# Linear attention and a GELU feed-forward layer: 192 bytes more ahead of one moving operand

## The chip, the cores and the metric

The kernel runs on 1 core of one Trainium2 chip, in one launch. The metric is device time in microseconds of that core, the median of the runs of a kernel.

## The reference

```
kv  = einsum('bhsd,bhse->bhde', k, v)          # 8 batches, 8 heads, seq 576, head_dim 64
out = einsum('bhsd,bhde->bhse', q, kv)
x   = out / sqrt(mean(out*out, -1) + 1e-6) * g_norm      # then heads side by side: (4608, 512)
h   = x @ w_in                                  # (512, 2048)
y   = gelu(h) @ w_out                           # (2048, 512); result (4608, 512)
```

All data are float32. The kernel splits each operand of the feed-forward layers into a high and a low part (hi and lo), and a product is hi·hi + lo·hi + hi·lo, three matmuls.

## The kernel before, in words

The 4608 tokens are cut into nine chunks of 512 (c = 0 to 8). The first two (PLAIN = 2) use the plain first layer, `layer1`. From c = 2 on the first layer uses Strassen's scheme with seven products per pair of feed-forward blocks: `layer1_pair` computes two of the 16 blocks of 128 features at once. One call of it is a *pair slot*; there are 7 chunks x 8 pairs = 56 of them. In a slot, `product(k, ...)` is called for k = 0 to 6, and each product issues 6 matmuls of 256 columns: two halves kb of the contraction, and for each the three terms (w hi, x hi), (w lo, x hi), (w hi, x lo). So a slot has 42 matmuls, all on line 444, and 56 slots have 2352. After a slot come the matmuls of the second layer (line 563, 512 columns), with the projections of the next chunk (line 218) between them in some slots. The order of the work is written out by hand (`manual_schedule`); the tile framework adds the waits.

A matmul has a *stationary* operand (weights, loaded into the array by an LDWEIGHTS of 128 columns, on the trace PEld) and a *moving* operand (streamed through, on the trace PE). While one matmul streams, the weights of the next are loaded. In `product` the weights come from a ring of four tiles w_in0 to w_in3, which the DMA queue of SyncE fills from DRAM (`load_products`), and the moving operand is `at.x[k]`, made by `high_block` (ScalarE cast, hi) and `low_block` (lo). For product 0 it lies in tile x2 (even c) or x0 (odd c); for product 1 in x3 or x1; for the others in tiles of the w_in family (`piece_tile`).

Where the operands lie is part of the program. The ring tiles have 64 elements (256 bytes) of room, and their contents start 48 elements (192 bytes) into the tile:

```
AWAY, ROOM = 48, 64
ring[t] = kept[t % RING][:, AWAY:AWAY + 2 * DM]
```

All other tiles start their contents at their first byte. As the program is built, the tiles named here begin, in each partition, at a byte address that leaves 192 when divided by 256 (x0 157888, x2 166080, w_in0 58560, w_in1 62912, w_in2 71360, w_in3 92096; the w_out, gh, gl and q tiles too). Pieces inside them begin at multiples of 512 bytes. In this text the *distance* of two operands is the start of the weights minus the start of the moving operand, taken modulo 256 bytes. It is 192 in all 42 matmuls of a slot, for a matmul's own weights and for the next ones alike; it is 0 in the second layer.

On the way to the prediction's steps: line 748 multiplies by an identity matrix (tile `ident`) at the start of the program; line 481 (`load_w`) issues the loads of the weights, w_in10 as the twentieth; lines 563 and 584 are the second layer and its very last part (`finish`), where the last row block is done in two halves of 256 columns.

Of the kernel before, what the change touches and what calls it, by code (L numbers as in the profile page):

```python
# [8 lines left out]
F32 = mybir.dt.float32  # L9
F32R = mybir.dt.float32r  # L10
# [6 lines left out]
P = 128  # L17
EPS = 1e-6
CH = 512
# [3 lines left out]
HALF = CH // 2  # L23
# [12 lines left out]
def linear_attn_rms_gelu_ffn(  # L36
# [16 lines left out]
    nc = tc.nc  # L53
    ctx.enter_context(tc.manual_schedule())
    NT, DM = out.shape
    B, NP = kv_main.shape[:2]
# [4 lines left out]
    NF = w_in.shape[0]  # L61
# [4 lines left out]
    const = ctx.enter_context(tc.tile_pool(name="const", bufs=1))  # L66
# [6 lines left out]
    HI, LO = slice(0, DM), slice(DM, 2 * DM)  # L73
    kv_h = [const.tile([P, NP, P], F32R, name=f"kv_h{s}") for s in range(2)]
    kv_l = [const.tile([P, NP, P], F32R, name=f"kv_l{s}") for s in range(2)]
    ident = const.tile([P, P], F32, name="ident")
    fold = const.tile([P, P], F32, name="fold")
    half_g = const.tile([P, 1], F32, name="half_g")
    heads = const.tile([P, 2], F32, name="heads")

    AWAY, ROOM = 48, 64

    def block_tile(name, dtype):
        ring = name in [f"w_in{i}" for i in range(RING)]
        return const.tile([P, 2 * DM + (ROOM if ring else 0)], dtype, name=name)


    kv_in, late = {}, {}  # L90

    def late_tile(name):

        if name not in late:
            late[name] = const.tile([P, 2 * DM], I32, name=name).bitcast(F32)
        return late[name]
# [77 lines left out]
    class Attn:  # L174
# [122 lines left out]
            self.low_x(p, eng)  # L297

        def high_x(self, p):
            x = const.tile([P, 2, CH], F32R, name=f"x{(NP * self.c + p) % 6}")  # L300
            nc.scalar.copy(out=x[:, 0], in_=self.o[p])
            self.x[p] = x

# [29 lines left out]
        def high_block(self, n):  # L333

            x = piece_tile(self.c, n)
            nc.scalar.copy(out=x[:, 0], in_=self.block(OPERANDS[n]))  # L336
            self.x[n] = x

        def low_block(self, n, eng=nc.gpsimd):
            x = self.x[n]  # L340
            eng.tensor_tensor(  # L341
                out=x[:, 1], in0=self.block(OPERANDS[n]), in1=x[:, 0].bitcast(F32),
                op=ALU.subtract,
            )

# [2 lines left out]
    OPERANDS = ((0, 0), "T1", "T2", "T4", (1, 0), (1, 1), "T3")  # L348
# [4 lines left out]
    def reused(i, dtype=F32):  # L353

        if i not in kept:
            kept[i] = block_tile(f"w_in{i}", dtype)
        return kept[i][:, :2 * DM]

    def piece_tile(c, n):
        k = (["x2", "x3"] + [f"w_in{i}" for i in range(5, 10)],  # L360
             ["x0", "x1", "x4", "x5"] + [f"w_in{i}" for i in range(10, 13)])[c % 2][n]
        return const.tile([P, 2, 2, HALF], F32R, name=k)

    products = [dram.tile([P, 2 * DM], F32, name=f"products{t}") for t in range(NT2)]

# [35 lines left out]
    def high_sums():  # L401

        for (j, second), s in stage.items():
            if j % 2:
                t = reused(second, F32R).rearrange("p (k a n) -> p k a n", k=2, a=2)
            else:
                t = const.tile([P, 2, 2, HALF], F32R, name=f"x{2 + second}")
            nc.scalar.copy(out=t[:, :, 0], in_=s)
            halved[j, second] = s, t
        stage.clear()  # L410
# [12 lines left out]
    def load_products(t):  # L423
        if t < (NCH - PLAIN) * NT2:
            reused(t % RING, F32R)
            ring[t] = kept[t % RING][:, AWAY:AWAY + 2 * DM]
            nc.sync.dma_start(out=ring[t].bitcast(F32), in_=products[t % NT2])

    def layer1_pair(at, j, between):


        a, b = (ps_h.tile([P, CH], F32, name="ps_h") for _ in range(2))
        left, right = slice(0, HALF), slice(HALF, CH)
        u = reused(15).rearrange("p (a n) -> p a n", n=HALF)
        p1, u2, v, u3 = (u[:, i] for i in range(4))
        add = lambda out, x, y: nc.vector.tensor_tensor(out=out, in0=x, in1=y, op=ALU.add)  # L436

        def product(k, out, first=False):
            n = ((at.c - PLAIN) * NF // 2 + j) * NPR + k
            w, x = ring[n // 2][:, n % 2 * DM:(n % 2 + 1) * DM], at.x[k]  # L440
            for kb in range(2):
                hi, lo = (w[:, m * HALF + kb * P:m * HALF + (kb + 1) * P] for m in range(2))
                for i, (y, z) in enumerate(((hi, 0), (lo, 0), (hi, 1))):
                    nc.tensor.matmul(  # L444
                        out=out, lhsT=y, rhs=x[:, z, kb], start=first and kb + i == 0,
                        stop=kb == 1 and i == 2, skip_group_check=True,
                    )
            if n % 2:
                load_products(n // 2 + RING)

        between[0]()
        product(0, a[:, left], True)
        product(1, a[:, right])
        nc.vector.tensor_copy(out=p1, in_=a[:, left])  # L454
        add(v, a[:, right], p1)
        product(2, b[:, right], True)
        product(3, b[:, left])
        add(u2, b[:, right], p1)
        between[1]()
        product(4, a[:, left])  # L460
        product(5, a[:, right])
        add(a[:, right], a[:, right], u2)
        product(6, b[:, right])
        add(u3, b[:, right], p1)
        add(b[:, left], b[:, left], u3)
        add(b[:, right], b[:, right], v)
        return a, b
# [9 lines left out]
    def load_w(n):  # L477
        kind, i = weights[n]
        src = w_in[i] if kind == "in" else w_out[i * P:(i + 1) * P, :]
        raw[n] = block_tile(f"w_{kind}{i}", I32)[:, :2 * DM]  # L480
        nc.sync.dma_start(out=raw[n], in_=src.bitcast(I32))
# [30 lines left out]
    def high_w(n):  # L512
        kind, i = weights[n]
        t = block_tile(f"w_{kind}{i}", F32R)[:, :2 * DM]
        parts[kind, i] = t
        nc.scalar.copy(out=t[:, HI], in_=ws[n].bitcast(F32))
# [90 lines left out]

    attn = [Attn(c) for c in range(NCH)]
    first, second = attn[:2]
    warm = late_tile(f"w_in{NF - 6}")[:, DM + P:DM + 2 * P]  # L610
    nc.vector.memset(warm, 0.0)
    nc.scalar.activation(out=heads, in_=warm[:, :2], func=AF.Gelu)
# [45 lines left out]
    for d in range(0, 2 * D, BLK):  # L658
        h = d // D * D
        nc.gpsimd.tensor_tensor(  # L660
            out=fold[:, d:d + BLK], in0=ident[:, h:h + BLK], in1=ident[:, h + BLK:h + 2 * BLK],
# [25 lines left out]
    n = 2 * NB  # L687


    def sum_squares(p):  # L690
# [10 lines left out]
        out=sums[:, :n + 4 * NG], lhsT=ones, rhs=eps[:, :n + 4 * NG], start=True, stop=False,  # L701
# [6 lines left out]
        out=half_g, in0=ps[:, :1], scalar1=0.5, scalar2=None, op0=ALU.mult  # L708
# [3 lines left out]
        out=root_g, in0=half_g, scalar1=D ** 0.5, scalar2=None, op0=ALU.mult  # L712
# [8 lines left out]
    for p in (2, 3):  # L721
# [5 lines left out]
        out=sums[:, :n].rearrange("p (g b) -> p g b", g=2), lhsT=fold, rhs=first.part[:, :2, :],  # L727
        start=False, stop=True, skip_group_check=True,
    )
    sum_squares(3)  # L730
    for p in (2, 3):
        nc.scalar.activation(
            out=first.o_tile(p), in_=first.ps.pop(p), func=AF.Copy, scale=root_g
# [9 lines left out]
    for p in (2, 3):  # L743
        bcs[p] = ps_acc.tile([P, DM], F32, name=f"acc{p}")
        for t in range(NG):
            for h, r in enumerate((slice(0, D), slice(D, 2 * D))):
                k = n + 2 * ((p - 2) * NG + t) + h
                nc.tensor.matmul(  # L748
                    out=bcs[p][r, t * P:(t + 1) * P],
                    lhsT=first.inv[:, k:k + 1].broadcast_to((P, D)), rhs=ident,  # L750
                    start=True, stop=True,
                )
    for p in range(2):
# [3 lines left out]
            out=first.o_tile(p), in0=first.ps.pop(p), scalar=root_g, in1=bc, op0=ALU.mult,  # L757
# [72 lines left out]
    def sum_weights(i, n, gelu_rest):  # L830

        high_sums()
        for k in range(n):
            if k:
                high_sums()
            combine(*halves.pop(0))
            if not k:
                gelu_rest()
            low_sums()
        if not n:  # L840
            gelu_rest()
            low_sums()
# [53 lines left out]
    for s in range(PLAIN * NF):  # L896
        c, i = divmod(s, NF)
# [35 lines left out]
        else:  # L933
# [3 lines left out]
            n = 0 if not 1 <= i <= 11 else 2 if i in (1, 3, 5, 7, 11) else 1  # L937
# [114 lines left out]
```

## Time and profile before

| | |
|---|---|
| median of 3 runs | 831.37 us (830.35 to 833.76) |
| the profiled execution, its own time | 831.25 us |
| its span, first to last instruction | 829.5 us |
| TensorE matmuls busy | 824.6 us (99% of the span) |
| weight loads busy (beside the matmuls) | 731.4 us (88%) |
| VectorE, ScalarE, GpSimd busy | 496.3, 314.0, 65.7 us |

The span is what the trace covers; 1.75 us of the execution's own time lie around it. A matmul's duration in the trace is longer than its pace, since matmuls are pipelined: what counts is the time from one start to the next.

### The profile page before, as it was taken

The numbers are of one execution on the slowest core, as the hardware profiler recorded it, in microseconds if no ns is written. First come the engines' busy times: TensorE is split into PE (matmuls) and PEld (weight loads), VectorE is DVE, ScalarE is ACT, GpSimd is POOL, SyncE is SP. The second block draws the span as 40 slices with busy tenths as digits, with TensorE's granted clock in tenths as the row PEclk, the third lists the DMA queues.
The fourth block names the chain that finished last, engine by engine and source line by source line (L and its number), as shares of the span: only waits on it lengthen the run. The fifth ranks groups of instructions, "written<-read, shape, count | busy, mean of one in ns | idle before, by whom it ended". The sixth has DMA issues, their size and how long they took to land.

```text
span 829.5 us, 13801 instructions
## 1 busy us (share of the span) xinstructions
PE 824.6 (99%) x5386; PEld 731.4 (88%) x5386; DVE 496.3 (60%) x980; ACT 314.0 (38%) x578; POOL 65.7 (8%) x69
## 2 busy tenths in 40 slices
PE   9999999999999999999999999999999999999998
PEld 7788888888999999999999999999999989999997
DVE  3899848677546744675457544673467456744443
ACT  3788544344431333233423253233423332322221
POOL 1000021002010100010100100010101000100000
PEclk9999999999999999999999999999999999999999
DMA  9981337777584578555845678456455655556551
GB/s 352 406 332 51 115 95 262 252 261 260 211 305 149 179 236 317 179 178 203 312 171 179 203 266 289 143 172 231 172 177 178 225 205 178 178 178 228 178 178 51
DMA packets 61605, 174.97 MB, mean 211 GB/s; under 512 B 6500, under 2 KB 15460, under 8 KB 61540
## 3 DMA queue, kind: packets, MB, share of 16 engines
q1 hardware_dynamic: 61536, 174.09, 60.4%
q8 instruction: 43, 0.70, 0.3%
q14 instruction: 22, 0.18, 0.1%
q10 hardware_dynamic: 4, 0.00, 0.0%
HBM read 149.95 MB, written 24.12 MB: 210 GB/s over the span
## 4 chain that ended last, share of the span: by engine, by line
PE 99%; DVE 0%; issue 0%; ACT 0%; DVEq 0%
PE acc L563 47%; PE ps_h L444 33%; PE ps_h L537 10%; PE ps_a L218 3%; PE ps_a L158 3%; PE ps_h L529 1%; PE ps_h L647 1%; PE acc L681 1%; PE acc L748 0%; PE ps_h L692 0%; PE ps_a L248 0%; DVE w L602 0%; DVE w_in L673 0%; PE ps_h L700 0%; DVE sq L591 0%
## 5 line engine op out<-in xcount | busy, mean ns | idle before, releaser
L563 PE MATMUL acc<-w_out,gh 128*128 128x512 f32 x700 | 216.7, 391 | 0.0
L444 PE MATMUL ps_h<-w_in,w_in 128*128 128x256 f32 x1392 | 173.0, 279 | 0.0
L444 PEld LDWEIGHTS ps_h<-w_in,w_in 128*128 128x128 f32 x1392 | 167.8, 188 | 0.0
L563 PE MATMUL acc<-w_out,w_in 128*128 128x512 f32 x672 | 159.3, 391 | 0.0
L563 PEld LDWEIGHTS acc<-w_out,gh 128*128 128x128 f32 x700 | 129.2, 188 | 25.3
L563 PEld LDWEIGHTS acc<-w_out,w_in 128*128 128x128 f32 x672 | 123.9, 188 | 24.6
L563 PE MATMUL acc<-w_out,gl 128*128 128x512 f32 x350 | 136.3, 389 | 0.0
L549 ACT ACTIVATE gh<-ps_h 128x512 fp32r<-128x512 f32 x88 | 52.7, 599 | 209.6 <-DVE ps_h L436 151.9
L444 PEld LDWEIGHTS ps_h<-x,w_in 128*128 128x128 f32 x960 | 120.9, 188 | 4.3
L444 PE MATMUL ps_h<-x,w_in 128*128 128x256 f32 x960 | 122.2, 279 | 0.0
L454 DVE COPY w_in<-ps_h 128x256 f32<-128x256 f32 x56 | 23.8, 425 | 131.6 <-PE ps_h L444 131.6
L549 ACT ACTIVATE w_in<-ps_h 128x512 fp32r<-128x512 f32 x56 | 33.6, 600 | 182.0 <-DVE ps_h L436 182.0
L436 DVE TENSOR_TENSOR ps_h<-ps_h,w_in 128x256 f32<-128x256 f32 x168 | 72.7, 433 | 46.1 <-PE ps_h L444 42.3
L436 DVE TENSOR_TENSOR w_in<-ps_h,w_in 128x256 f32<-128x256 f32 x168 | 71.4, 425 | 46.8 <-PE ps_h L444 44.9
L537 PE MATMUL ps_h<-x,w_in 128*128 128x512 f32 x360 | 86.8, 390 | 0.0
L555 DVE TENSOR_TENSOR gl<-ps_h,gh 128x512 fp32r<-128x512 f32 x88 | 60.4, 687 | 43.0 <-ACT ps_h L550 38.7
L550 ACT ACTIVATE ps_h<-ps_h 128x512 f32<-128x512 f32 x144 | 85.5, 594 | 0.0
L537 PEld LDWEIGHTS ps_h<-x,w_in 128*128 128x128 f32 x360 | 67.4, 188 | 13.9 <-POOL x L306 0.2
L563 PEld LDWEIGHTS acc<-w_out,gl 128*128 128x128 f32 x350 | 65.7, 188 | 13.9
L555 DVE TENSOR_TENSOR w_in<-ps_h,w_in 128x512 fp32r<-128x512 f32 x56 | 38.4, 686 | 17.1 <-ACT ps_h L550 17.1
L206 POOL TENSOR_TENSOR ql<-q,qh 128x512 fp32r<-128x512 f32 x16 | 21.3, 1331 | 210.6 <-ACT qh L205 152.9
L341 POOL TENSOR_TENSOR w_in<-o,w_in 128x512 fp32r<-128x512 f32 x13 | 17.0, 1325 | 208.1 <-ACT w_in L336 208.1
(153 smaller groups left out, 644.1 us busy)
## 6 DMA issues: line engine op xcount, KB each, us to landing
w_in<-products SPq DMA_DIRECT2D x196, 512.0 KB, 4.6
products<-w_in SPq DMA_DIRECT2D x40, 256.0 KB, 3.2
w_in<-w_in SPq DMA_DIRECT2D x16, 512.0 KB, 10.2
kv_main<-kv_main SPq DMA_DIRECT2D x16, 512.0 KB, 7.1
w_out<-w_out SPq DMA_DIRECT2D x16, 512.0 KB, 10.2
q<-qT SPq DMA_DIRECT2D x15, 512.0 KB, 6.0
out<-w SPq DMA_DIRECT2D x18, 256.0 KB, 2.1
out<-z SPq DMA_DIRECT2D x17, 256.0 KB, 2.3
```

What stands on the lines that cost most here:

```text
L158: nc.tensor.matmul(out=ps[r, n * D:(n + 1) * D], lhsT=k[:, r], rhs=v[:, r], start=(j == 0), stop=(j == NJ),)
L206: eng.tensor_tensor(out=ql, in0=q, in1=qh.bitcast(F32), op=ALU.subtract)
L218: nc.tensor.matmul(out=ps[:, a:e], lhsT=w, rhs=x[:, a:e], start=(m == 0), stop=(m == 2))
L341: eng.tensor_tensor(out=x[:, 1], in0=self.block(OPERANDS[n]), in1=x[:, 0].bitcast(F32), op=ALU.subtract,)
L436: add = lambda out, x, y: nc.vector.tensor_tensor(out=out, in0=x, in1=y, op=ALU.add)
L444: nc.tensor.matmul(out=out, lhsT=y, rhs=x[:, z, kb], start=first and kb + i == 0, stop=kb == 1 and i == 2, skip_group_check=True,)
L454: nc.vector.tensor_copy(out=p1, in_=a[:, left])
L537: nc.tensor.matmul(out=h, lhsT=parts["in", i][:, w][:, p * P:(p + 1) * P], rhs=at.x[p][:, x], start=(m + p == 0), stop=(m == 2 and p == NP ...
L549: nc.scalar.activation(out=gh, in_=h, func=AF.Gelu)
L550: nc.scalar.activation(out=h, in_=h, func=AF.Gelu)
L555: nc.vector.tensor_tensor(out=gl, in0=h, in1=gh.bitcast(F32), op=ALU.subtract)
L563: nc.tensor.matmul(out=ps, lhsT=x[:, ts], rhs=parts["out", i][:, w], start=(i == 0 and m == 0), stop=(m == 2 and (i == NF - 1 or (i, t) == ...
```

## The change

The tiles x0 and x2 get 64 more elements (256 bytes). When a tile holds the first product's operand (`n == 0` in `piece_tile`), its hi part starts 48 elements into the tile, with a gap of 16 elements between its two halves kb, and its lo part starts at element 576. So hi kb = 0 begins at byte 192, hi kb = 1 at byte 1280, lo at bytes 2304 and 3328: only the first of these four quarters leaves another remainder modulo 256. The operand becomes a pair of slices (`x[0]`, `x[1]`) in place of one tile with an axis for hi and lo. The 512 bytes that the two tiles take come from `ident`, which has no tile of its own any more: it lies in a part of w_in10 that is unused until that tile's weights are loaded.

```diff
-    ident = const.tile([P, P], F32, name="ident")
...
+    def x_tile(i):
+        return const.tile([P, 2 * DM + (ROOM if i in (0, 2) else 0)], F32R, name=f"x{i}")
...
         def high_x(self, p):
-            x = const.tile([P, 2, CH], F32R, name=f"x{(NP * self.c + p) % 6}")
+            x = x_tile((NP * self.c + p) % 6)[:, :2 * CH].rearrange("p (a n) -> p a n", a=2)
...
         def high_block(self, n):
             x = piece_tile(self.c, n)
-            nc.scalar.copy(out=x[:, 0], in_=self.block(OPERANDS[n]))
+            nc.scalar.copy(out=x[0], in_=self.block(OPERANDS[n]))
...
     def piece_tile(c, n):
         k = (["x2", "x3"] + [f"w_in{i}" for i in range(5, 10)],
              ["x0", "x1", "x4", "x5"] + [f"w_in{i}" for i in range(10, 13)])[c % 2][n]
-        return const.tile([P, 2, 2, HALF], F32R, name=k)
+        t = const.tile([P, 2 * DM], F32R, name=k) if k[0] == "w" else x_tile(int(k[1]))
+        if n:
+            hi, lo = t[:, :DM], t[:, DM:2 * DM]
+        else:
+            hi, lo = t[:, AWAY:AWAY + DM + 2 * (ROOM - AWAY)], t[:, DM + ROOM:]
+        return tuple(a.rearrange("p (k n) -> p k n", k=2)[:, :, :HALF] for a in (hi, lo))
...
                     nc.tensor.matmul(
-                        out=out, lhsT=y, rhs=x[:, z, kb], start=first and kb + i == 0,
+                        out=out, lhsT=y, rhs=x[z][:, kb], start=first and kb + i == 0,
...
+    ident = late_tile(f"w_in{NF - 6}")[:, DM + 2 * P:DM + 3 * P]
```

No instruction is added, removed or moved on any engine. In the built program the x0 and x2 tiles, the w_in tiles and the w_out tiles lie 512 bytes (x1 and x2: 256 bytes) lower than before, so their remainders modulo 256 stay at 192. The distances of a slot's 42 matmuls after the change: 0 for the first two (w hi and w lo with x hi, kb = 0), 192 for the other 40. Two kinds of wait change: the load of w_in10 waits for the last matmul of line 748 instead of an earlier one, and for GpSimd's work on `fold` instead of its memsets before. In seven ScalarE casts (`high_block(0)`, once a chunk) the output is two pieces of 256 elements with a gap.

## Rows read from the trace of the kernel before

**Rows 1.** The page: busy time, granted clock by slices, the chain that ended last.
```profile
PE 824.6 (99%) x5386; PEld 731.4 (88%) x5386; DVE 496.3 (60%) x980; ACT 314.0 (38%) x578; POOL 65.7 (8%) x69
...
PEclk9999999999999999999999999999999999999999
...
PE 99%; DVE 0%; issue 0%; ACT 0%; DVEq 0%
PE acc L563 47%; PE ps_h L444 33%; PE ps_h L537 10%; PE ps_a L218 3%; PE ps_a L158 3%; PE ps_h L529 1%; PE ps_h L647 1%; PE acc L681 1%; PE acc L748 0%; PE ps_h L692 0%; PE ps_a L248 0%; DVE w L602 0%; DVE w_in L673 0%; PE ps_h L700 0%; DVE sq L591 0%
```
**Rows 2.** Timeline of PE, first pair slot: start us, us, engine, line, operation, count.
```profile
209.78 0.39 PE L563 MATMUL acc<-w_out,gl 128*128 128x512 f32 x1
210.01 1.57 PE L444 MATMUL ps_h<-x,w_in 128*128 128x256 f32 x12
211.42 3.70 PE L444 MATMUL ps_h<-w_in,w_in 128*128 128x256 f32 x30
214.95 0.25 PE L218 MATMUL ps_a<-qh,kv_h 128*128 128x192 f32 x1
```
**Rows 3.** Timeline of PE, a slot of the last chunk.
```profile
737.42 1.58 PE L444 MATMUL ps_h<-x,w_in 128*128 128x256 f32 x12
738.83 3.69 PE L444 MATMUL ps_h<-w_in,w_in 128*128 128x256 f32 x30
742.36 0.63 PE L563 MATMUL acc<-w_out,gh 128*128 128x512 f32 x2
```
**Rows 4.** Stretches of line 444: length, PE busy, PEld busy, granted clock, DMA share, GB/s.
```profile
209.90:214.80 4.90, 4.79 (x41) 4.86 (x42) 1.00 0.40 116
737.30:742.20 4.90, 4.78 (x41) 4.86 (x42) 1.00 0.45 118
```
**Rows 5.** Timeline of PE, the last matmuls of the program.
```profile
824.65 0.40 PE L584 MATMUL acc<-w_out,gh 128*128 128x256 f32 x2
824.88 0.28 PE L584 MATMUL acc<-w_out,gl 128*128 128x256 f32 x1
825.00 0.40 PE L584 MATMUL acc<-w_out,gh 128*128 128x256 f32 x2
825.24 0.28 PE L584 MATMUL acc<-w_out,gl 128*128 128x256 f32 x1
825.36 0.40 PE L584 MATMUL ps_h<-w_out,gh 128*128 128x256 f32 x2
...
825.96 0.28 PE L584 MATMUL ps_h<-w_out,gl 128*128 128x256 f32 x1
```
**Rows 6.** Timeline of PE, projections of 256 columns (first and last of six).
```profile
301.43 0.28 PE L218 MATMUL ps_a<-qh,kv_h 128*128 128x256 f32 x1
...
302.02 0.28 PE L218 MATMUL ps_a<-ql,kv_h 128*128 128x256 f32 x1
```
**Rows 7.** Timeline of PE, second layer right behind a projection.
```profile
215.72 0.62 PE L563 MATMUL acc<-w_out,gh 128*128 128x512 f32 x2
...
217.11 0.62 PE L563 MATMUL acc<-w_out,gh 128*128 128x512 f32 x2
...
217.79 0.62 PE L563 MATMUL acc<-w_out,gh 128*128 128x512 f32 x2
```
**Rows 8.** Timelines of PE (identity matmuls) and of the SyncE queue (load of w_in10).
```profile
19.74 2.15 PE L748 MATMUL acc<-ident,y 128*64 128x128 f32 x32
...
38.74 0.33 SPq L481 DMA_DIRECT2D w_in<-w_in  x1
```
**Rows 9.** ACT groups, shapes apart: busy us, mean ns, idle before and releaser.
```profile
L336 ACT CAST x<-o 128x512 fp32r<-128x512 f32 x14 | 8.7, 619 | 13.1 <-DVE o L289 12.6 <-ACT ps_h L550 0.5
...
L408 ACT CAST x<-w 128x512 fp32r<-128x512 f32 x8 | 4.8, 610 | 4.2 <-DVE w L398 4.2
```

More of the change, by code (lines that the diff above doesn't have):

```diff
@@ L341, in low_block @@
             eng.tensor_tensor(
-                out=x[:, 1], in0=self.block(OPERANDS[n]), in1=x[:, 0].bitcast(F32),
+                out=x[1], in0=self.block(OPERANDS[n]), in1=x[0].bitcast(F32),
                 op=ALU.subtract,
@@ L406, in high_sums @@
             else:
-                t = const.tile([P, 2, 2, HALF], F32R, name=f"x{2 + second}")
+                t = x_tile(2 + second)[:, :2 * DM]
+                t = t.rearrange("p (k a n) -> p k a n", k=2, a=2)
             nc.scalar.copy(out=t[:, :, 0], in_=s)
```

## The prediction

> **What bounds the kernel now.** I read the page first. TensorE's matmuls are busy for 824.6 of 829.5 us, and the chain that ended last is 99% TensorE, 33% of the span of it on line 444, the matmuls of the pair slots [rows 1]. The granted clock is at its upper level, 2.4 GHz, in every slice of the page, and 1.00 in the stretches of two slots [rows 1, 4]. So the time is the sum of the paces at which TensorE starts its matmuls. A change that moves no instruction can act in two ways: through that pace, or through a new wait on TensorE.
>
> The pace is read from starts in the timeline. In the first slot 12 matmuls on the x tiles (products 0 and 1) take from 210.01 to 211.42, 1.41 us or 117.5 ns each; the 30 of products 2 to 6 take from 211.42 to 214.95, 3.53 us or 117.7 ns each. The whole slot is 4.94 us, 117.6 ns a matmul [rows 2]. A slot of the last chunk gives the same: 1.41 us, then 3.53 us, 4.94 us in all [rows 3]. 56 slots of 4.94 us are 276.6 us, one third of the span, as the chain says. The reader is to see in this how even it is. The matmuls that the change touches stand in the first group of 12, and that group is no slower than the other 30: there is no stall at the head of a slot that a better address could take away. It shows a second thing: products 0 and 1 read their weights from the first ring tile and the others from three more, which lie at different multiples of 256 bytes, and the pace is the same. That is why I count addresses modulo 256.
>
> **What the distance is worth, from rows.** The change takes the distance from 192 to 0 for two of a slot's 42 matmuls, 2 x 56 = 112 in all. Do matmuls of 256 columns run at another pace at distance 0? The slots don't show it, but the very last part of the program does: on line 584 the weights gh, gl and the moving w_out both begin at remainder 192. Its first two intervals go from 824.65 to 824.88, 0.23 us or 115 ns each. From there nine intervals go to 825.96, 1.08 us or 120.0 ns each [rows 5]. So distance 0, coming out of a run of 512-column matmuls as a slot does, starts a little faster than a slot's 117.6 and settles a little slower. The counterpart at distance 192 is on line 218: the kv tiles begin at remainder 128, the q tiles at 192, so the distance is 192 too, and five intervals from 301.43 to 302.02 take 0.59 us, 118 ns each, as in a slot [rows 6].
>
> Line 584 has other tiles than a slot, so this is the nearest row and no direct proof. By it each distance has a pace that it settles to, 117.6 at 192 and 120.0 at 0, and the way there lasts a few matmuls.
>
> **The Trainium skill against this.** The page "TensorE: Matmul & The Clock Gate", section "Step-by-step: what each phase is for", says that TensorE has two independent read ports, one for the moving operand and one for the weights, and that loading the next weights takes no read bandwidth from the matmul that runs. By that rule no distance matters, the change is worth nothing, and the time stays at 831.4 us. The rows differ from it by 2.4 ns a matmul (120.0 against 117.6), a hint and no more; no run here has yet put one operand at two distances. I keep the rule as a rival.
>
> **The terms of the sum.**
> 1. The two matmuls at distance 0. The head of a slot takes 2 x 117.6 = 0.235 us now. Bounds: 0.23 us, if it goes as the head of line 584, or 0.240 us, at the settled 120.0 ns [rows 2, 5]. Over 56 slots that is -0.28 to +0.27 us. I take -0.3 us, because the situation (two matmuls right behind 512-column ones) is that of the head of line 584.
> 2. What the other 40 do after that. If the pace depends on distance and on what went before, the disturbance can go on for some matmuls. How long such a thing lasts is shown by the second layer: right behind a projection, six intervals of 512-column matmuls go from 215.72 to 217.11, 1.39 us, while the next three take 0.68 us, 226.7 ns each, so that six settled ones take 1.36 us [rows 7]. The disturbance costs 0.03 us and is gone after six matmuls. As much at every slot, with either sign, is 56 x 0.03 = 1.7 us. I take 0: line 218 comes out of another kind of neighbour and is at 118 ns at once [rows 6], and a slot is too. The 1.7 us stay in the range.
> 3. The load of w_in10 now waits for the identity matmuls. They end at 19.74 + 2.15 = 21.89 us; that load is issued at 38.74 us [rows 8], 16.9 us later, in a queue that is behind older loads. Cost 0. Were the cover gone, the load and those behind it in the queue would be late by the difference.
> 4. The identity matmuls get another address as well: 2.15 us for 32 [rows 8]. At 5 ns each way they give 0.16 us at most; I take 0.
> 5. Seven casts write two pieces. The cast takes 619 ns; one on line 408, which already writes two separated pieces, takes 610 [rows 9], and ScalarE is busy 38% of the span [rows 1]. Cost 0; 10 ns more would hide in the 13.1 us for which ScalarE waits ahead of such casts.
> 6. The other tiles move by 256 or 512 bytes, and no remainder changes. Cost 0, by the four ring tiles above.
>
> Sum: -0.3 us on the execution's own 831.25, that is 830.95. The median of the runs shown stands 0.12 above it, so the forecast is 831.1 us. The runs shown spread from 830.35 to 833.76; half a per cent, 4.2 us, is about what a measurement can tell from no change, and I use it as the bound of "same".
>
> **Rivals.**
> *The head of the slot sets the pace of the whole slot (faster).* If the two matmuls at distance 0 put the weight loads and the stream into another alignment, and distance 192 holds that alignment, the fast pace of the head of line 584 could last: 115 against 117.6 ns for 42 matmuls is 0.11 us a slot, 6.1 us, giving 825.1 us. For it speaks that one and the same distance does show two paces, 115 at first and 120 later, so there is a memory [rows 5, 7]. Against it: in every stretch I read, the memory fades within about six matmuls, and 56 slots and line 218 all stand at the same pace after different neighbours. It counts as faster from 4.2 us / 2352 matmuls = 1.8 ns each, a slot of 4.87 us or less.
>
> *The settled pace of distance 0 holds for the slot (slower).* The same mechanism with the other sign: the slot goes on at 120.0 ns, 42 x 2.4 ns = 0.10 us a slot, 5.6 us over 56, giving 837.0 us. For it: 120.0 is the pace at which nine intervals in a row stand [rows 5]. Against it: 40 of 42 matmuls keep distance 192, whose settled pace is 117.6, and two at distance 0 have not yet got to 120 on line 584. It decides from 119.4 ns a matmul, a slot of 5.02 us.
>
> *The distance does nothing (same).* Rows 2, 3 and 6 are then simply what matmuls of 256 columns take, and line 584 is slower for another reason; 831.4 us. By the page's rule above it would be this.
>
> **How the numbers follow.** The forecast, with terms 1 and 2, has 0.60; that distance does nothing has 0.14; both lie within 0.5% and make "same" 0.74. The fast slot has 0.18: that a fast alignment exists is seen, that it lasts is not. The slow slot has 0.08. The likeliest case's own range is 831.1 with 1.7 us of term 2 and the spread of medians, 829 to 833.6. To leave out no more than 2 in 10 the range must reach one of the other cases; the fast slot is the likelier, so it goes down to 825.0; the slow one is left out.
>
> **What would show it.** In the timeline of the changed kernel the first slot's 12 matmuls on x tiles should take 1.40 to 1.42 us and the next 30 3.53; the granted clock should stay 1.00 there, and no wait should stand ahead of line 444. Right about the head but wrong about the rest would be a group of 30 that takes 3.45 us (115 ns) or 3.60 us (120 ns). The prediction is wrong if the pace of all 42 changes by 1.8 ns or more, which the memory after a short disturbance would have to carry over 40 matmuls; or if the time moves in a place that these rows don't speak of.

## The result, and the profile after

The changed kernel is slower: 834.40 us (median of 8 runs, 832.82 to 836.51) against 831.25 us (8 runs), a ratio of 1.0038 with a 95% interval of 1.0021 to 1.0055. The forecast was 831.1 us, in a range of 825.0 to 833.6, with "same" (less than half a per cent) as the likeliest. By that bound the outcome is still "same", but it is slower clear of the noise, and the time lies outside the range. Measured again beside the experiments below, the same kernel gave 833.13 against 830.97 us, 1.0027 (1.0013 to 1.0042), which lies inside it.

The page of the changed kernel (rows that answer to [rows 1]):

```profile
span 833.7 us, 13801 instructions
...
PE 828.7 (99%) x5386; PEld 733.0 (88%) x5386; DVE 496.0 (59%) x980; ACT 314.1 (38%) x578; POOL 65.6 (8%) x69
...
PE 97%; DMA 2%; SPq 0%; DVE 0%; issue 0%; ACT 0%; DVEq 0%
```

The span is 4.2 us longer, and TensorE is still busy for 99% of it. The 2% of the chain on DMA come from the one wait of TensorE that is new, 0.22 us for a load of kv_main at the start of the program:

```profile
18.23 1.12 PE L161 MATMUL ps_a<-kv_main 112*64 112x64 f32 x16 [0.22 <-DMA kv_main<-kv_main]
```

From the first slot on TensorE waits for nothing, before and after. So the question is again at which pace TensorE starts its matmuls, and where it got slower. The timeline of PE answers, first at the first pair slot (as [rows 2]; line 444 is now 454, line 563 is 573):

```profile
212.05 0.39 PE L573 MATMUL acc<-w_out,gl 128*128 128x512 f32 x1
212.28 1.57 PE L454 MATMUL ps_h<-x,w_in 128*128 128x256 f32 x12
213.69 3.69 PE L454 MATMUL ps_h<-w_in,w_in 128*128 128x256 f32 x30
217.22 0.25 PE L221 MATMUL ps_a<-qh,kv_h 128*128 128x192 f32 x1
```

Two things stand there. The slot starts 2.27 us later than before (212.28 against 210.01): that much of the 4.2 us was lost before any slot had used an operand at a new distance. And the slot is as long as before: 1.41, then 3.53 us, 4.94 in all. The other 2 us must have been lost between slots.

They were lost right behind them. A slot of the last chunk that is followed by 13 matmuls of the second layer in one row shows it. The kernel before:

```profile
768.60 1.58 PE L444 MATMUL ps_h<-x,w_in 128*128 128x256 f32 x12
770.01 3.69 PE L444 MATMUL ps_h<-w_in,w_in 128*128 128x256 f32 x30
773.54 3.12 PE L563 MATMUL acc<-w_out,w_in 128*128 128x512 f32 x13
```

The changed one, same slot:

```profile
772.59 1.57 PE L454 MATMUL ps_h<-x,w_in 128*128 128x256 f32 x12
774.00 3.70 PE L454 MATMUL ps_h<-w_in,w_in 128*128 128x256 f32 x30
777.53 3.17 PE L573 MATMUL acc<-w_out,w_in 128*128 128x512 f32 x13
```

The slot takes 4.94 us in both, and the same 13 matmuls behind it, whose operands the change does not touch, take 3.17 us in place of 3.12. Resolved into single intervals, from one start to the next in the two traces, in ns (the head as a mean of the 56 slots; the slot's last interval and the second layer behind it for the slot shown):

```
                    head of a slot (mean of 56)         last  second layer behind it
before              117.4 118.3 117.5 117.5 118.3 ...   115   233 231 226 227 227 226 227 227 226 227 227
changed             115.8 118.4 117.5 117.5 117.5 ...   118   241 237 233 236 224 231 236 228 233 231 226
```

The first interval of a slot is 1.6 ns shorter; after it the slot keeps the old pace, 117.8 ns in the mean. But the second layer now needs ten intervals to settle at 226.7 ns, where it needed two. Summed over the trace by stretches, the 56 slots are 0.14 us shorter and the stretches behind them 2.12 us longer: 55 to 56 ns behind each of the 35 slots that are followed at once by the second layer or by projections of 256 columns, 49 ns behind 3 where these have 512 columns, and next to nothing (-11 to +10 ns) behind the 18 slots where other work follows. From the first slot's first matmul to the last matmul's start it is 617.94 us against 615.95, 1.99 us or 0.24%.

The other 2.3 us belong to the start, and to the executions that were profiled. The identity matmuls, in the changed kernel's two profiled executions (the first in the result, the second among the experiments):

```profile
20.22 3.68 PE L759 MATMUL acc<-w_in,y 128*64 128x128 f32 x32
```
```profile
18.23 1.97 PE L759 MATMUL acc<-w_in,y 128*64 128x128 f32 x32
```

and the windows around them, with the granted clock behind the count; the third is of the kernel before, whose identity matmuls took 2.15 us [rows 8]:

```profile
18.00:22.00 4.00, 3.78 (x42) 0.50 1.03 405
```
```profile
18.00:22.00 4.00, 3.96 (x38) 1.00 1.04 409
```
```profile
18.00:22.00 4.00, 4.00 (x57) 0.73 1.02 399
```

In the first, TensorE ran this stretch at the lower clock, 1.2 GHz (0.50); in the second at 2.4 GHz (1.00); the kernel before had both (0.73). The first two had short waits for data ahead of it: TensorE was busy for 3.87 and 3.90 of the 4.00 us from 10 to 14 us. The same program shows both starts, so the lower clock does not come with the program. It makes the spreads wide: the five runs of the first measurement at a mean clock of 1.00 lie at 832.8 to 833.3 us but for one at 836.5, the three at 0.996 at 835.5 to 836.4. Whether the change makes such a start more frequent is open: the mean granted clock was 0.998 or less in 8 of 20 executions of the changed kernel, and in 13 of the 58 of the kernel before beside the experiments.

### The profile page after: what moved, and what is told of

Its sections match the earlier page's. It is cut to its first block, busy times and chain, and to the rows that moved or that the text cites. A ratio compares the mean times of both kernels' runs of the same rounds, so it can differ in the third digit from the quotient of the medians.

```text
span 833.7 us, 13801 instructions
## 1 busy us (share of the span) xinstructions
PE 828.7 (99%) x5386; PEld 733.0 (88%) x5386; DVE 496.0 (59%) x980; ACT 314.1 (38%) x578; POOL 65.6 (8%) x69
## 4 chain that ended last, share of the span: by engine, by line
PE 97%; DMA 2%; SPq 0%; DVE 0%; issue 0%; ACT 0%; DVEq 0%
PE acc L573 47%; PE ps_h L454 33%; PE ps_h L547 10%; PE ps_a L221 3%; PE ps_a L161 2%; DMA kv_main<-kv_main 1%; PE ps_h L539 1%; DMA w_in<-qT 1%; PE acc L759 0%; PE ps_a L251 0%; SPq L127 0%; PE ps_h L658 0%; DVE w L612 0%; DVE sq L601 0%; DVE z L602 0%; SPq L189 0%
```

## The experiments

**Again.** The changed kernel, unedited.

> The changed kernel once more, to separate what its trace shows twice from what one execution shows. Theory A (the two matmuls at distance 0 leave TensorE in another alignment, which the next 40 matmuls carry at an unchanged pace and the second layer behind the slot pays for, about 56 ns in 36 slots and 49 ns in 3): again 2.1 us more on the second-layer line behind the slots, whatever the start of the program does. Theory B (the start of the program is slower, because the identity matrix has moved into w_in10): the identity matmuls take 3.7 us again and not 2.15. Theory C (chance): the start goes back to 2.15 us. A and C together give 833.2 us, A and B 834.8 us.

833.13 us against 830.97 (12 and 29 runs). From the first slot to the end it is 617.94 us, the same as in the first profile to 0.01 us, with 241, 238, 233, 236, 224, ... behind the slots; the start is quick. Theories A and C hold; B, as a start that is slow every time, falls.

**Room only.** All of the change but the shift:

```diff
-            hi, lo = t[:, AWAY:AWAY + DM + 2 * (ROOM - AWAY)], t[:, DM + ROOM:]
+            hi, lo = t[:, :DM], t[:, DM + ROOM:]
```

> Everything of the change (larger x0 and x2, identity matrix in w_in10, all tiles 256 or 512 bytes lower) but the shift itself: the first product's hi part begins at byte 0, so all 42 matmuls of a slot are at distance 192. Theory A: the second layer behind a slot starts as before (233, 231, then 226.5 ns), time as before, 831.2 us. Theory B (start) or theory D (the second layer meets other addresses, since the w_out tiles moved by 512 bytes against gh and gl): slower as the changed kernel, 833 to 834.5 us; D shows it on the second-layer line, B in the identity matmuls.

831.71 us, ratio 1.0012 (0.9998 to 1.0026). The timeline of the slot shown above:

```profile
767.68 1.58 PE L454 MATMUL ps_h<-x,w_in 128*128 128x256 f32 x12
769.09 3.69 PE L454 MATMUL ps_h<-w_in,w_in 128*128 128x256 f32 x30
772.62 3.12 PE L573 MATMUL acc<-w_out,w_in 128*128 128x512 f32 x13
```

3.12 us behind the slot, and 615.95 us from the first slot to the end, as before. So the larger tiles and the 512 bytes by which other tiles moved cost nothing from the first slot on. Ahead of it, with the granted clock at 1.00, the identity matmuls take 1.97 us with the matrix in w_in10 (room only) and in a tile of its own (the last experiment below):

```profile
18.90 1.97 PE L759 MATMUL acc<-w_in,y 128*64 128x128 f32 x32
```
```profile
18.39 1.97 PE L758 MATMUL acc<-ident,y 128*64 128x128 f32 x32
```

Theories B and D fall. The 2 us from the first slot on are the shift's.

**Late pair.** The shift in product 6 in place of product 0 (the room goes to w_in9 and w_in12, its tiles):

```diff
...
-        if n:
+        if n != 6:
             hi, lo = t[:, :DM], t[:, DM:2 * DM]
...
```

> The shift by 192 bytes sits in product 6 in place of product 0, so matmuls 37 and 38 of a slot are at distance 0 and the other 40 at 192. Theory A, if the alignment only has to be left once and is then kept: the second layer behind a slot pays the same 56 ns, 833.2 us. If what counts is how long the slot runs on after the pair (4 matmuls here, 40 in the changed kernel), the cost differs: between 0 and 100 ns a slot, 831 to 836 us. Theories B and D: as room_only.

830.93 us, ratio 1.0000 (0.9986 to 1.0014).

```profile
774.88 3.12 PE L573 MATMUL acc<-w_out,w_in 128*128 128x512 f32 x13
```

Nothing: the two intervals take 117.5 and 118.3 ns, the second layer starts as before, 615.95 us. My expectation of a cost either way was wrong. As matmuls 37 and 38 of a slot, two matmuls at distance 0 leave no cost; at its head they leave one that comes 40 matmuls later.

**Ring at 0.** The kernel before with all 42 matmuls at distance 0:

```diff
-    AWAY, ROOM = 48, 64
+    AWAY, ROOM = 0, 64
```

> The kernel before with the ring's contents at byte 0 of their tiles: all 42 matmuls of a slot at distance 0. By the settled pace of the last part of the program (120.0 ns) a slot takes 5.04 us in place of 4.94, 5.6 us more in all: 836.9 us. If distance has no part in the pace: 4.94 us a slot and 831.3 us.

835.88 us, ratio 1.0067 (1.0043 to 1.0091).

```profile
776.32 1.59 PE L444 MATMUL ps_h<-x,w_in 128*128 128x256 f32 x12
777.75 3.76 PE L444 MATMUL ps_h<-w_in,w_in 128*128 128x256 f32 x30
781.36 3.14 PE L563 MATMUL acc<-w_out,w_in 128*128 128x512 f32 x13
```

By these rounded starts that is 3.61 us for 30; by the single ones it is 120.0 ns each. So distance does set the pace, at the size that the last lines of the kernel before had shown [rows 5], head included (113.2, 119.2, then 120.0 ns here; 113, 119, then 120 there). From the first slot to the end it is 5.5 us longer, 4.9 in the slots and 0.6 behind them; 5.6 were expected in the slots. In another row of this trace stood what I had not looked for. These are the projections behind the ninth slot, first and last of six, at distance 192:

```profile
305.04 0.28 PE L218 MATMUL ps_a<-qh,kv_h 128*128 128x256 f32 x1
...
305.61 0.28 PE L218 MATMUL ps_a<-ql,kv_h 128*128 128x256 f32 x1
```

Five intervals in 0.57 us, 113 to 114 ns each. The same five intervals take 0.59 us before [rows 6]. One distance has two paces.

**First only, second only.** The order of product 0's terms is changed, so that only one of the head's matmuls is at distance 0; the other comes sixth.

```diff
...
+            terms = [(kb, m, z) for kb in range(2) for m, z in ((0, 0), (1, 0), (0, 1))]
+            if k == 0:
+                terms = [terms[i] for i in (0, 2, 3, 4, 5, 1)]      # second only: (2, 0, 3, 4, 5, 1)
...
```

> The changed kernel with the six terms of product 0 in another order, so that of the head's matmuls only the first is at distance 0 (the other one comes sixth). Theory A2 (the first interval of a slot decides: at distance 0 it lasts 115.8 ns and not 117.5, TensorE gets a lead there, and 41 matmuls at distance 192 keep it at an unchanged pace; a pair in the middle of a slot can't do that): first interval about 115.8, second layer behind the slot 56 ns dearer, as in the changed kernel. Rival A3 (two in a row at distance 0 are needed): the second layer starts as before, 233, 231, 226.

> The terms of product 0 in the order (w hi, x lo), (w hi, x hi), ..., so that the slot's second matmul is at distance 0 and its first at 192. Theory A2: first interval 117.5 ns, no lead, the second layer behind the slot as before (233, 231, 226). Rival A3b (the second of the two does it): 56 ns dearer.

One run each: 829.82 and 831.01 us beside 830.95 before. In these and in all single runs below I go by the length from the first slot to the end. First only has the short first interval (115.9 ns), but after some uneven ones (115.8, 121.6, 117.5, 115.9, 120.0) the slot is as long as before and the second layer starts at 232, 231, 227: 615.95 us, no cost. That is not what theory A2 expects, though the matmul that comes sixth, at distance 0, may have undone what the first had done, so this run alone is not clean. Second only gains 6.6 ns a slot, most of it in the interval right behind the one that comes sixth (112.5 ns), and has the old start of the second layer, 615.58 us.

**64 and 128 bytes in place of 192.** The first two matmuls at distance 128 (first16) or 64 (first32):

```diff
-            hi, lo = t[:, AWAY:AWAY + DM + 2 * (ROOM - AWAY)], t[:, DM + ROOM:]
+            hi, lo = t[:, 32:32 + DM + 2 * (ROOM - 32)], t[:, DM + ROOM:]      # first16: 16
```

> The changed kernel with 128 bytes in place of 192 ahead of the first product's operand: the first two matmuls of a slot are at distance 64. Theory A2: what counts is the length of the first interval; if it is 117.5 again, the second layer starts as before, if it is near 115.8 or shorter, it pays 50 ns or more a slot. Rival A4 (any break of the even distance at the head does it): 56 ns whatever the first interval is.

> The same with 64 bytes: the first two matmuls of a slot at distance 128. Theory A2 and rival A4 as for first32: the first interval's length against the second layer's start.

One run each: 831.54 and 830.96 us beside 830.95. First16 has the same short first interval as the changed kernel, 115.8 ns, and no cost (615.95 us): after 119.2, 123.3 and 112.5 ns the slot is where it always was. First32 starts with 116.7 ns and pays 37 to 39 ns behind 35 slots, 617.34 us. So theory A2 falls, and A4 too: neither the length of the first interval nor a break as such decides.

**Six.** All of product 0's moving operand is shifted:

```diff
-            hi, lo = t[:, AWAY:AWAY + DM + 2 * (ROOM - AWAY)], t[:, DM + ROOM:]
+            hi, lo = t[:, AWAY:AWAY + DM], t[:, AWAY + DM:AWAY + 2 * DM]
```

> The changed kernel with both halves of hi and of lo of the first product 192 bytes into the tile: the first six matmuls of a slot at distance 0, the other 36 at 192. In ring0 the six projections behind a slot at distance 0 (they are at distance 192) ran at 113.3 ns each and not at 118. Theory E (distance 192 has two paces, and a run of matmuls at distance 0 ahead, settled at 120.0, puts the stream on the faster one, which it keeps): 36 x 4.5 ns less a slot, about 8 us less in all, 822.5 to 824 us. Rival F (the fast pace lasts some matmuls only, or needs the projections' operands): 117.8 ns again after a few matmuls, 830.5 to 833.5 us.

832.47 us, ratio 1.0030 (1.0019 to 1.0040), 617.71 us from the first slot.

```profile
770.74 3.69 PE L454 MATMUL ps_h<-w_in,w_in 128*128 128x256 f32 x30
774.27 3.16 PE L573 MATMUL acc<-w_out,w_in 128*128 128x512 f32 x13
```

The head does come to 120.0 ns (three intervals), but the 30 that follow take 3.53 us, 117.7 ns each, and the second layer pays. Theory E fails in this form.

**Ring at 128 and at 64 bytes.** The kernel before with `AWAY` 32 or 16, all 42 matmuls at distance 128 or 64.

> The kernel before with the ring's contents at byte 128: all 42 matmuls at distance 128. No row shows a settled pace at this distance. Between 113.3 ns (the fastest that a run of 256-column matmuls has shown) and 120.0 ns: a slot of 4.76 to 5.04 us, 820.5 to 836.9 us. Theory E says that each distance has its own settled paces; if only 0 is apart, 117.8.

> The same with the ring's contents at byte 64: all 42 matmuls at distance 64. Bounds as for ring32: 113.3 to 120.0 ns a matmul, 820.5 to 836.9 us.

One run each: 838.25 and 834.33 us beside 830.55 before. At distance 128 a matmul takes 117.5, 120.0 and 122.5 ns in turn, 120.0 in the mean (623.26 us from the first slot); at 64 it takes 117.8, and 38 slots are followed by 19 to 47 ns more (616.83 us). Of the four distances 192 is the best as long as the head is left alone.

**Product 0's weights at 0.** From the kernel before: the weights of product 0 move, not its moving operand. The head's operands then lie at the remainders that they had in ring0, and the other 36 matmuls at distance 192.

```diff
-            ring[t] = kept[t % RING][:, AWAY:AWAY + 2 * DM]
-            nc.sync.dma_start(out=ring[t].bitcast(F32), in_=products[t % NT2])
+            heads0 = [(2 * t + a) % NPR in (0,) for a in range(2)]
+            at = (0 if heads0[0] else AWAY, DM + (ROOM if heads0[1] else AWAY))
+            ring[t] = [kept[t % RING][:, o:o + DM] for o in at]
...
+                for a in range(2):
+                    nc.sync.dma_start(
+                        out=ring[t][a].bitcast(F32), in_=products[t % NT2][:, a * DM:(a + 1) * DM]
+                    )
```

> The kernel before, with the weights of product 0 (not its moving operand) moved: they lie at byte 0 of their ring tile, or 256 bytes on in its second half, so a slot's first six matmuls are at distance 0 with the same remainders as in ring0, where the head took 113.2, 119.2, then 120.0 ns, and the matmuls at distance 192 behind the slot 113.3 ns. The other 36 are at 192. The tiles that hold a product 0 are loaded by two transfers. Theory E2 (what decides is the alignment that the head leaves, and this head leaves the one that ring0 does, in which distance 192 runs at 113.3 ns for as long as it goes on): 36 x 4.4 ns less a slot, 8.7 us in all, 822 to 824 us. Rival F (113.3 ns lasts some matmuls only): 117.8 ns again within a slot, 829.5 to 833 us.

823.14 us against 831.16, ratio 0.9908 (0.9889 to 0.9928): faster than both kernels. The page and the same slot:

```profile
span 820.1 us, 13895 instructions
```
```profile
759.86 1.56 PE L454 MATMUL ps_h<-x,w_in 128*128 128x256 f32 x12
761.25 3.56 PE L454 MATMUL ps_h<-w_in,w_in 128*128 128x256 f32 x30
764.65 3.14 PE L573 MATMUL acc<-w_out,w_in 128*128 128x512 f32 x13
```

30 matmuls in 3.40 us, 113.3 ns each, at distance 192, where the kernel before takes 3.53 us. The intervals are 113.2, 119.2, 120.0, 120.0, 120.0, 120.8 and then 113.3 to the end of the slot. The slots are 8.35 us shorter in all and the stretches behind them 0.39 us longer, 607.99 us from the first slot. Theory E2 expected 8.7 less and 822 to 824 us. Rival F, that the fast pace lasts for some matmuls only, falls.

## Why the prediction was wrong

The step that failed is term 2, "What the other 40 do after that", which I took at 0 because a disturbance "is gone after six matmuls" [rows 7]. The rows were right, but they are of 512-column matmuls in the second layer. In a slot the disturbance of the head does not fade: it is carried through 40 matmuls at a pace that cannot be told from the old one, and shows when the second layer begins, at 49 to 56 ns behind 38 slots, 2.10 us, and 2.12 us behind all 56. Room only takes the shift away and with it the cost; late pair puts the shift at another place and has none. The 1.7 us that I kept for this term in the range were near its size by luck: they stood for another disturbance, in another place and of another duration. I had looked for a cost of the head in the slot, and listed as signs of an error a different length of the 30 matmuls; neither came. The sign that came is the last one that I gave, time that moves in a place that these rows do not speak of.

Point by point:

- *Term 1*, the two matmuls themselves, -0.28 to +0.27 us, taken as -0.3: measured -0.09 us in these two intervals and -0.14 us over the slots.
- *Terms 3 to 6*, the load of w_in10, the identity matmuls, the casts, the moved tiles, at 0: right, as far as the traces go. Room only has all of them but the casts: its identity matmuls take 1.97 us, like those of a tile of their own, and it stands at 615.95 us from the first slot. The casts take 618 ns in the changed kernel, 619 before. The load of w_in10 is issued at 38.57 us in the changed kernel, 38.74 before. The slow start of the profiled execution does not need them: ring0, with the identity matrix in its own tile, shows identity matmuls of 3.68 us as well. But I had misread the start. The page shows the clock as 9 in every slice, which stands for 90% and more, and a slice is 20.7 us long; within the first two, from 14 to 22 us, the kernel before was granted 0.84 and 0.73. The 2.15 us of term 4 were a mixture of both clocks, and the sum had no term for a start at the lower one.
- *Distance does nothing* (the rival beside which I cited the Trainium skill): false. The same matmuls take 113.3, 117.8 and 120.0 ns with operands at other addresses. The Trainium skill, "TensorE: Matmul & The Clock Gate", section "Step-by-step: what each phase is for", says that loading the next weights takes no read bandwidth from the running matmul. That no distance matters was my inference from it, and these runs, in which nothing but addresses (and, in product0_zero, the cut of some transfers) differs, do not bear it out; whether a load takes read bandwidth they do not show.
- *The fast slot*: the changed kernel does not reach it, but my reason against it was wrong. I argued that the memory fades in every stretch; product0_zero keeps a pace of 113.3 ns for 36 matmuls. I priced it at 115 ns and 6.1 us; it is 113.3 ns and gives 8.0 us in the time (8.35 in the slots). With that falls what I had read from the even pace of a slot, that no better address at its head could take time away.
- *The slow slot*, 120.0 ns throughout: did not come, for the reason given. Slower came by a way that I had not priced as a rival: an unchanged slot with a dearer start of the work behind it.
- *The range*: 834.40 lies 0.8 us above its upper end. Of the 3.3 us to the forecast, 2.0 are this cost. The rest fits the start of the program described above; that it is only this was not shown. The cost alone, added to the forecast, is 833.1 us and inside the range, as the second measurement is. So what the range missed by is the start; what the mechanism had wrong is term 2.

What the head decides, then, is a state in which one distance has several settled forms. That it exists and lasts is shown by the runs. That it is an alignment of the weight loads and the moving stream, as the theories say, is an argument: in the starts of the traces it cannot be seen, since within a slot a matmul begins 115 to 116 ns after its weight load both before and after the change (110 ns in product0_zero, 117 in ring0). Which address sets it was not settled: six and product0_zero both put six matmuls at distance 0 and both come to 120.0 ns, but only the second goes on to 113.3. They differ in the remainders of the weights and of the moving operand, and so also in the distance between the slot's first weights and the second-layer operand that streams while these are loaded (192 in six, 0 in product0_zero). That this is the reason is an argument; no run changes it alone.

## What to carry to other kernels

A pace that stays the same does not mean that the state stays the same: after a change of operand addresses, compare the first intervals of the next stretch too, down to single starts. When one row of a trace shows the same matmul at two paces (here 113 and 118 ns), look for what came ahead of it; that row was worth 1% of the kernel, and the change itself 0.3% the other way. And separate the start of a program from its body before a difference of 0.3% is explained: here the clock at the start moved the first slot of one execution by more than the change moved all that followed (2.27 us against 1.99).

## What the runs showed of the hardware that I had not expected

- A run of 256-column matmuls has settled paces that depend on the operands' distance modulo 256 bytes and on what came ahead: 120.0 ns at 0, 117.8 at 64, 120.0 at 128 (117.5, 120.0 and 122.5 in turn), 117.8 or 113.3 at 192. In the runs that move the ring only the weights' address differs; that the distance counts and not this address alone rests on six, where the moving operand moved and the head came to 120.0 as well.
- The trace gives a slot's weight loads 187 to 188 ns at distance 192, at either pace, and 192 ns at distance 0 (ring0).
- The starts of the second layer behind the slots are all the end of one series. The changed kernel runs through the whole of it: 241, 237, 233, 236, 224, 231, 236, 228, 233, 231 ns, then 226.7. First32 and six enter it one step further on (235, then 233 or 234, 236, 224, ...), ring32 two (233, 236, 224, ...); ring16, ring0 and product0_zero begin with 233 and go on with its last four (236, 228 or 229, 232, 231), and the kernel before has its last two (233, 231). What a slot hands on shows as the place where the second layer enters; above 226.7 ns each, the whole series costs 63 ns and the last two intervals 10.
- The settled paces fit a grid of 6.67 ns: 113.3 is 17 of it, 120.0 is 18, the 512-column pace of 226.7 is 34, and three matmuls at 117.8 are 53. Some of these starts fit it too. Against the kernel before, a slot is shifted by 0.0 ns in first16 and by -6.6 in second only, and both have the old start of the second layer; it is shifted by 1.7 ns in first32 and by 8.5 in six, 6.8 apart, and these two have one and the same other start. The changed kernel stands at -2.4 and has a third one. But product0_zero, at -149.1, stands at -2.4 too, but for 22 such steps, and does not have the changed kernel's start. So the shift alone does not settle it, and what in the chip has this period no run here tells.
